# Attention and a max-out MoE layer in one kernel: batch 0 cut into two query parts, with MoE spans of 256 and 320 tokens

## The chip, the core and the metric

The kernel runs on one core of one Trainium2 chip. The metric is the device time of one execution in microseconds. Seven runs of the kernel before the change have a median of 294.08 us (293.69 to 296.04).

## What is computed

```python
def _attn_ref(q, k, v):                       # (8, 8, 576, 64) each: batch, head, sequence, dim
    scores = 1.0 / np.sqrt(D) * np.matmul(q, k.transpose(0, 1, 3, 2))
    mask = (pos[:, None] // 64) >= (pos[None, :] // 64)
    scores = np.where(mask, scores, -1000000000.0)
    attn = np.exp(scores - np.max(scores, axis=-1, keepdims=True))
    attn = attn / (np.sum(attn, axis=-1, keepdims=True) + 1e-09)
    return np.matmul(attn, v)

x = attn_out.transpose(0, 2, 1, 3).reshape(4608, 512)
g = np.maximum(x @ w1, x @ w2)                # w1, w2: (512, 1024)
out = g @ w_out                               # w_out: (1024, 512), out: (4608, 512)
```

The mask is causal by blocks of 64: a query sees all keys of its own block and of the blocks ahead of it. All inputs are float32; the kernel computes in bfloat16 with float32 accumulation.

## The kernel before

**Attention.** The heads of a batch are worked on two at a time: 4 pairs a batch, 32 pairs in all (`NPAIR`). Two pairs make a group g, and q and k of a group are loaded together (`load_qk`, L89, by SP), cast to bfloat16 (`cast`, L101), transposed on TensorE (`transposes`, L259) and copied out of PSUM into rings of four (`qT_r`, `kT_r`). For a pair, TensorE computes transposed scores (`scores`, L278: keys on partitions, queries in columns), 128 keys (a chunk, 5 in all) at a time and only for queries that can see them. ACT takes the exponential into `aT` (`exp`, L287). Where the first 64 queries of a chunk's columns must not see its last 64 keys, GpSimd writes zeros (`mask`, L292: 64 partitions, 2 x 64 elements; four a pair). `burst_a` (L295) and `burst_b` (L306) do the two halves of a pair; each uses two of the two buffers of the PSUM pool `ps_s`, so a score tile waits until ACT has read the one two before it. `CB` (L50) says where in `aT` a chunk begins.

`av` (L317) multiplies `aT` with V, which has a column of ones for the row sums, for some query tiles of 128 (tiles 0 and 1, or 2 to 4), and DVE divides by the sum (L339, L340). `x_out` (L345) transposes a group's result on TensorE, and DVE copies it into `xT` (L358, L359), the MoE's input with features on partitions. After a batch's second group `done_tokens` rises by 576.

**MoE.** Tokens are cut into 9 spans of 512. `h_unit(i, f)` (L159) computes 128 of the 1024 hidden features of span i: 4 matmuls with w1, a copy on DVE (L175), 4 with w2 and a maximum on DVE (L177). `y_unit` (L181) multiplies 128 tokens of the result g with w_out (8 matmuls), ACT copies it out (L192), and SP stores it. `y_last` does the last 128 tokens in halves. The PSUM pool `ps_m` has 4 buffers for everything but scores.

**Order.** The order on each engine is that in which the Python code issues (L70, `manual_schedule`); nothing is moved later. The MoE is a generator of single matmul steps (`moe`, L216). `fill(n)` (L245) takes up to n steps of it, but only those whose span lies within `done_tokens` (`needs`, `ready`). The main loop (L455) goes over pairs 4 to 31 and puts fills between the bursts; `fill_of` (L368) divides the steps that are ready, less 6, over the pairs until more come. AV of a pair follows two pairs later (`LAG`).

**The start** (L416 to L452). Batch 0 has no MoE beside it. Its four pairs run one after the other, with `warm_up` matmuls on zeros between (L251); then come AV of pairs 1 to 3, `x_out(0)` and `x_out(1)`. Only then is the first span ready. In the loop's first pass (s == HP) 6 steps, the transposes of group 2 and 6 more steps come first.

**Loads.** q and k of groups 0 to 2 are issued at once by SP (and ACT, for the first k). GpSimd issues what is cast on the way: five V chunks a batch (`load_v`, L107), w1 and w2 in quarters and a half (`load_w`, L118) and w_out (`load_wo`). q and k of later groups are gated: GpSimd first writes one column of the target (L94), and SP's load waits for that. So GpSimd's queue, which also holds masks and most casts (`pool_work`, L375), sets when they start.

Of the kernel before, what the change touches and what calls it, by code (L numbers as in the profile page):

```python
# [14 lines left out]
def kernel(  # L15
# [36 lines left out]
    APAD = 64  # L52
    NCH = 5

    SPAN = 512
    NSPAN = NTOK // SPAN

    wpool = ctx.enter_context(tc.tile_pool(name="wpool", bufs=1))
    ring = ctx.enter_context(tc.tile_pool(name="ring", bufs=1))
# [29 lines left out]
    def load_qk(g, queues, gated=False):  # L89
        b, u = divmod(g, GPB)  # L90
        for nm, src, queue in (("q", q, queues[0]), ("k", k, queues[1])):
            raws[nm, g] = t = raw.tile([P, 2, RPP * D], FP32, name=f"{nm}raw")
            if gated:
                nc.gpsimd.memset(t[:, 0, :1], 0.0)  # L94
            queue.dma_start(
                out=t[:],
                in_=src[b, 4 * u:4 * u + 4].rearrange(
                    "(s h) (p t) d -> (h p) s (t d)", h=2, t=RPP),
            )
# [15 lines left out]
    w2r = moe_w2.rearrange("(c p) f -> p c f", p=P)  # L115
    wor = moe_w_out.rearrange("(c p) f -> p c f", p=P)

    def load_w(f0, fw):  # L118
        for dst, src in ((w1_sb, w1r), (w2_sb, w2r)):
            nc.gpsimd.dma_start(out=dst[:, :, f0:f0 + fw], in_=src[:, :, f0:f0 + fw])  # L120

    def load_wo(c0, n):
        nc.gpsimd.dma_start(out=wo_sb[:, c0:c0 + n, :], in_=wor[:, c0:c0 + n, :])
# [8 lines left out]
    nc.vector.memset(zeros[:], 0.0)  # L132
    nc.scalar.activation(out=warm[:], in_=warm[:], func=AF.Exp)
    load_qk(1, (SP, SP))
    load_qk(2, (SP, SP))
    make_identity(nc, ident)
    for r in range(NV):
        nc.vector.memset(vv_r[r][:, :, :, D:D + 1], 1.0)
# [3 lines left out]
    for r in range(NA):  # L142
        nc.vector.memset(aT_r[r][BLK:, :, CB[4] + 512:], 0.0)
        nc.vector.memset(aT_r[r][:BLK, :, AW:], 0.0)
    cast("q", 0, ((dve, 0, 6), (pool, 6, RPP)))
    cast("k", 0, ((act, 0, 5), (dve, 5, RPP)))
    for c in range(3):
        load_v(0, c)
    cast("q", 1, ((pool, 0, RPP),))
    for c in range(3, NCH):  # L150
        load_v(0, c)
    load_w(0, 256)
    load_w(256, 256)


    done_tokens = [0]
# [1 line left out]

    def h_unit(i, f):  # L159
        if f == 0:  # L160
            g_tiles[i] = g_pool.tile([P, NFF, SPAN], BF16, name="g")
        g = g_tiles[i]
        t0 = i * SPAN
        ph = []
        for w_sb in (w1_sb, w2_sb):
            pt = ps_m.tile([P, SPAN], FP32, name="ps_h", tag="m")
            for c in range(NDM):
                nc.tensor.matmul(  # L168
                    pt[:], w_sb[:, c, f * P:(f + 1) * P], xT[:, c, t0:t0 + SPAN],
                    start=(c == 0), stop=(c == NDM - 1),  # L170
                )
                if c == NDM - 1:
                    if not ph:
                        h1 = h1_pool.tile([P, SPAN], BF16, name="h1")
                        nc.vector.tensor_copy(out=h1[:], in_=pt[:])  # L175
                    else:
                        nc.vector.tensor_max(g[:, f, :], h1[:], pt[:])  # L177
                    ph.append(pt)
                yield

    def y_unit(i, s):  # L181
        g = g_tiles[i]
        t0 = i * SPAN + s * P
        py = ps_m.tile([P, d_model], FP32, name="ps_y", tag="m")
        for f in range(NFF):
            nc.tensor.matmul(  # L186
                py[:], g[:, f, s * P:(s + 1) * P], wo_sb[:, f, :],
                start=(f == 0), stop=(f == NFF - 1),
            )
            if f == NFF - 1:  # L190
                y = y_pool.tile([P, d_model], FP32, name="y")
                nc.scalar.copy(out=y[:], in_=py[:])  # L192
                nc.sync.dma_start(out=out[t0:t0 + P, :], in_=y[:])
            yield

    def y_last(i, s):
        g = g_tiles[i]
        t0 = i * SPAN + s * P
        w = d_model // 2
        for h in range(2):  # L200
            py = ps_m.tile([P, w], FP32, name="ps_y", tag="m")
# [11 lines left out]
                            out=out[t0:t0 + P, h * w + m:h * w + m + w // 2], in_=y[:])  # L213
                yield

    def moe():  # L216
        ny = SPAN // P
        for i in range(NSPAN):
            need = (i + 1) * SPAN
            for f in range(NFF):  # L220
                yield from ((need, 0) for _ in h_unit(i, f))
                if i > 1 and f % 2 == 0:
                    yield from ((need, 0) for _ in y_unit(i - 1, f // 2))
            if i == 0:
                for s in range(ny):
                    yield from ((need, 0) for _ in y_unit(0, s))
        for s in range(ny - 1):
            yield from ((NTOK, 0) for _ in y_unit(NSPAN - 1, s))
        yield from ((NTOK, 0) for _ in y_last(NSPAN - 1, ny - 1))


    needs = []
    for i in range(NSPAN):
        needs += [(i + 1) * SPAN] * (2 * NDM * NFF + (SPAN // P * NFF if i != 1 else 0))
    needs += [NTOK] * ((SPAN // P + 1) * NFF)
    moe_steps = moe()
    at = [0]

    def ready():
        n = at[0]  # L240
        while n < len(needs) and needs[n] <= done_tokens[0]:
            n += 1
        return n - at[0]

    def fill(n):  # L245
        for _ in range(min(n, ready())):
            next(moe_steps)
            at[0] += 1


# [38 lines left out]
            out=aT_r[p % NA][:m, :, a0:a0 + w], in_=ps[:m, :, :w], func=AF.Exp, scale=scale,  # L289
        )  # L290

    def mask(p, a0):  # L292
        nc.gpsimd.memset(aT_r[p % NA][BLK:, :, a0:a0 + BLK], 0.0)  # L293

    def burst_a(p):  # L295
        u0 = ps_s.tile([P, 2, 512], FP32, name="ps_s", tag="s")
# [20 lines left out]
    def av(p, ts):  # L317
# [11 lines left out]
        for gi, t in enumerate(ts):  # L329
            for hh in range(2):  # L330
                for c in range(t + 1):
                    a0 = CB[c] + t * P
                    nc.tensor.matmul(  # L333
                        po[:, gi, hh, :], a[:, hh, a0:a0 + P], vv[:, c, h0 + 2 * hh, :],
                        start=(mm == 0), stop=(mm == n_mm - 1),
                    )
                    mm += 1
# [4 lines left out]
            rec[:, :n].to_broadcast([P, n, 2, D]),  # L342
        )

    def x_out(g):  # L345
        b, u = divmod(g, GPB)
        xp = xps.pop(g)
        pe = ps_m.tile([P, 2, NCH, BLK], BF16, name="ps_xe", tag="m")
        po = ps_m.tile([P, 2, NCH - 1, BLK], BF16, name="ps_xo", tag="m")
        for s in range(2):  # L350
            for t in range(NCH):
                src = xp[:, t, s].rearrange("p a d -> p (a d)")
                nc.tensor.transpose(pe[:, s, t, :], src[:BLK], ident[:BLK, :BLK])  # L353
                if t < NCH - 1:
                    nc.tensor.transpose(po[:, s, t, :], src[BLK:], ident[BLK:, BLK:])
        dst = xT[:, 2 * u:2 * u + 2, b * S:b * S + NCH * P].rearrange(
            "p s (t h w) -> p s t h w", h=2, w=BLK)
        nc.vector.tensor_copy(out=dst[:, :, :, 0], in_=pe[:])  # L358
        nc.vector.tensor_copy(out=dst[:, :, :NCH - 1, 1], in_=po[:])  # L359
        if u == GPB - 1:  # L360
            done_tokens[0] = (b + 1) * S

# [9 lines left out]

    def pool_work(s):  # L375
        g, i = divmod(s, 2)
        if s == 0:
            load_w(512, 512)
            load_qk(3, (SP, SP), gated=True)
        elif s == 1 or s == 2:  # L380
            pass
        elif s == 3:
            cast("q", 2, ((act, 0, RPP),))
            cast("k", 2, ((act, 0, RPP),))
            load_qk(4, (SP, SP), gated=True)
            for c in range(3):
                load_v(1, c)
            cast("q", 3, ((pool, 0, RPP),))
            cast("k", 3, ((pool, 0, RPP),))
            for c in range(3, NCH):  # L390
                load_v(1, c)
            load_wo(0, 4)
            load_wo(4, 4)
        elif s == 4:
            pass
        elif s == 5:
            load_qk(5, (SP, SP), gated=True)
# [24 lines left out]
    ck((0,))  # L422
    cq((1,))
    ck((1,))
    for s in range(HP):
        burst_a(s)
        if s == 0:
            cast("k", 1, ((dve, 0, RPP),))
            warm_up(4)
        elif s == 1:  # L430
            transposes("k", 1, (dve, dve))()
            warm_up(2)
        elif s == 2:
            av(0, [0, 1])
            warm_up(2)
        else:
            av(0, [2, 3, 4])
        burst_b(s)
        pool_work(s)
        if s == 0:  # L440
            transposes("q", 1, (dve, dve))()
            warm_up(2)
        elif s == 1:
            warm_up(4)
        elif s == 2:
            warm_up(3)
    for p in (1, 2, 3):
        av(p, [0, 1])
        av(p, [2, 3, 4])
        if p == 2:  # L450
            x_out(0)
    x_out(1)  # L452

    x_due = []
    for s in range(HP, NPAIR):  # L455
        g, i = divmod(s, 2)
        if x_due:
            x_out(x_due.pop())
        n = fill_of(s)
        if s == HP:  # L460
            fill(6)
            cq = transposes("q", 2, (dve, act))
            ck = transposes("k", 2, (dve, act))
            cq()
            ck()
            fill(6)
        burst_a(s)
        n_a = n // 2 if n > 12 else n * 2 // 5
        n_b = n // 6
# [5 lines left out]
        if s >= HP + LAG:  # L475
            p = s - LAG
            av(p, [0, 1])
            fill(n_b)
            av(p, [2, 3, 4])
            if p % 2:  # L480
                x_due.append(p // 2)
        else:
            fill(n_b)
        fill(n - n_a - n_b)
# [5 lines left out]
        av(p, [2, 3, 4])  # L490
        fill(11)
    x_out(NG - 1)
    fill(len(needs))

# [33 lines left out]
```

The softmax here doesn't subtract the row's maximum and nothing guards it: scores larger than these inputs give would overflow.

## Time and profile before

| | |
|---|---|
| median of 7 runs | 294.08 us |
| profiled execution | 294.02 us |
| its span | 292.2 us |
| TensorE clock granted | 1.0 of full speed |
| HBM read, written | 34.60 MB, 9.44 MB |
| L168 ps_h matmuls | 133.6 us busy, 379 ns each |
| L186 ps_y matmuls | 66.5 us busy |
| L288 exponentials | 99.1 us busy |
| L109 V loads issued by GpSimd | 33.7 us busy |

The span is the time from the first to the last instruction in one profiled execution; 1.8 us lie around it. Engines are named PE (TensorE matmul), PEld (its weight loads), DVE, ACT, POOL (GpSimd) and SP. Matmuls overlap, so the 379 ns of one is longer than the distance to the next. An arrow `<-` in square brackets names what ended an engine's idle time before an instruction. For a DMA, "to landing" is the time from its issue until its data is there.

### The profile page before, as it was taken

Reading aid. Unit: us, or ns where it says so; the run is one execution under the profiler, and the core shown is the slowest. Engines: PE = TensorE matmul, PEld = TensorE weight load, DVE = VectorE, ACT = ScalarE, POOL = GpSimd, SP = SyncE. Lnnn points to the kernel's source line nnn. Section 1 sums busy time; section 2 is a strip of 40 time slices with the busy share of each in tenths; the row PEclk is TensorE's granted clock in tenths of the full one; section 3 lists DMA queues with packets and bytes.
Section 4 is the critical chain, followed back from the end, with each engine's and each line's share of the span. In section 5 each row is a group of like instructions: output and inputs, shape, how many; then the busy total and the mean of one; then the engine's idle time right before and its main releaser. Section 6 shows DMA issues by size and latency. Waiting matters only on the chain.

```text
span 292.2 us, 7406 instructions
## 1 busy us (share of the span) xinstructions
PE 277.0 (95%) x3067; PEld 141.1 (48%) x3116; DVE 181.8 (62%) x363; ACT 140.2 (48%) x200; POOL 95.5 (33%) x236
## 2 busy tenths in 40 slices
PE   8787999999999999999999999999999999999995
PEld 3345445445554454544454455454545544444443
DVE  6717677547986676666565656666665766464530
ACT  3883687686655555554545555545555000101112
POOL 2956536625644443144324432443111000000000
PEclk9999999999999999999999999999999999999999
DMA  7999999968923792569556594465110111011104
GB/s 264 289 187 294 222 183 169 235 145 170 201 31 145 94 216 46 199 73 211 73 200 72 145 139 148 81 62 63 40 38 37 38 69 41 36 72 38 72 36 144
DMA packets 56081, 36.65 MB, mean 125 GB/s; under 512 B 38768, under 2 KB 43376, under 8 KB 56048
## 3 DMA queue, kind: packets, MB, share of 16 engines
q0 software_dynamic: 41728, 7.87, 34.1%
q1 hardware_dynamic: 13760, 27.60, 27.9%
q10 hardware_dynamic: 560, 0.72, 0.7%
q8 instruction: 24, 0.39, 0.5%
q14 instruction: 9, 0.07, 0.1%
HBM read 34.60 MB, written 9.44 MB: 151 GB/s over the span
## 4 chain that ended last, share of the span: by engine, by line
PE 90%; ACT 4%; DVE 3%; issue 2%; ACTq 0%
PE ps_h L168 42%; PE ps_y L186 20%; PE ps_o L333 11%; PE ps_s L282 8%; ACT aT L288 3%; PE ps_w L254 3%; PE ps_qT L265 2%; PE ps_kT L265 2%; PE ps_xe L353 2%; DVE xp L340 1%; PE ps_y L203 1%; DVE kT L272 1%; DVE xT L358 0%; DVE qT L272 0%; DVE rec L339 0%
## 5 line engine op out<-in xcount | busy, mean ns | idle before, releaser
L168 PE MATMUL ps_h<-xT,w_sb 128*128 128x512 bf16 x547 | 133.6, 379 | 3.5 <-issue 1.8
L288 ACT ACTIVATE aT<-ps_s 128x1024 bf16<-128x1024 f32 (+1 forms) x128 | 99.1, 832 | 53.5 <-PE ps_s L282 53.5
L168 PEld LDWEIGHTS <-w_sb 128*128 128x128 bf16 x576 | 51.8, 98 | 59.7 <-issue 6.1
L175 DVE CAST h<-ps_h 128x512 bf16<-128x512 f32 x72 | 49.7, 690 | 45.0 <-PE ps_h L168 44.1
L186 PE MATMUL ps_y<-wo_sb,g 128*128 128x512 bf16 x262 | 66.5, 379 | 1.0 <-issue 0.2
L293 POOL MEMSET aT<- 64x128 bf16 x128 | 23.5, 199 | 120.7 <-ACT aT L288 120.5
L192 ACT COPY y<-ps_y 128x512 f32<-128x512 f32 x35 | 20.5, 587 | 83.9 <-PE ps_y L186 56.8
L177 DVE TENSOR_TENSOR g<-h,ps_h 128x512 bf16<-128x512 bf16 x72 | 49.3, 684 | 10.2 <-PE ps_h L168 10.2
L333 PEld LDWEIGHTS <-aT 128*128 128x128 bf16 x960 | 33.6, 98 | 14.9 <-DVE xp L340 8.4
L333 PE MATMUL ps_o<-vv,aT 128*128 128x65 bf16 x960 | 39.7, 194 | 1.1 <-DVE xp L340 0.4
L186 PEld LDWEIGHTS <-g 128*128 128x128 bf16 x280 | 25.5, 98 | 27.9 <-issue 3.2
L282 PE MATMUL ps_s<-qT,kT 64*128 64x64 bf16 (+4 forms) x384 | 34.5, 275 | 3.3 <-ACT aT L288 3.2
L109 POOL DMA_DIRECT2D vv<-in_v_dram x40 | 33.7, 848 | 0.3 <-issue 0.3
L340 DVE TENSOR_TENSOR xp<-ps_o,rec 128x256 bf16<-128x256 f32 x64 | 31.4, 491 | 2.2
L282 PEld LDWEIGHTS <-kT 64*128 64x128 bf16 x384 | 16.5, 94 | 18.9 <-issue 13.2
L339 DVE RECIPROCAL rec<-ps_o 128x4 f32<-128x4 f32 x64 | 11.8, 184 | 18.9 <-PE ps_o L333 18.8
L105 POOL CAST qn<-qraw 128x1152 bf16<-128x1152 f32 (+1 forms) x15 | 17.1, 1137 | 4.6 <-DMA qraw<-in_q_dram 4.6
L272 DVE COPY qT<-ps_qT 128x576 bf16<-128x576 bf16 x17 | 12.8, 757 | 5.6 <-PE ps_qT L265 4.4
L105 POOL CAST kn<-kraw 128x1152 bf16<-128x1152 f32 x13 | 14.9, 1144 | 2.2 <-DMA kraw<-in_k_dram 1.4
L358 DVE COPY xT<-ps_xe 128x640 bf16<-128x640 bf16 x16 | 7.8, 490 | 12.5 <-PE ps_xe L353 12.1
L272 DVE COPY kT<-ps_kT 128x576 bf16<-128x576 bf16 x17 | 12.8, 756 | 4.3 <-PE ps_kT L265 3.3
L254 PE MATMUL ps_w<-zeros 128*128 128x512 bf16 x34 | 10.9, 451 | 1.8 <-DVE zeros L132 1.2
(39 smaller groups left out, 102.8 us busy)
## 6 DMA issues: line engine op xcount, KB each, us to landing
qraw<-in_q_dram SPq DMA_DIRECT2D x16, 576.0 KB, 4.4
out_dram<-y SPq DMA_DIRECT2D x35, 256.0 KB, 2.1
kraw<-in_k_dram SPq DMA_DIRECT2D x15, 576.0 KB, 6.1
vv<-in_v_dram POOLq DMA_DIRECT2D x32, 128.0 KB, 5.7
w_sb<-in_moe_w_dram POOLq DMA_DIRECT2D x4, 256.0 KB, 7.6
w_sb<-in_moe_w_dram POOLq DMA_DIRECT2D x2, 512.0 KB, 16.4
wo_sb<-in_moe_w_out_dram POOLq DMA_DIRECT2D x2, 512.0 KB, 12.2
kraw<-in_k_dram ACTq DMA_DIRECT2D x1, 576.0 KB, 5.6
```

Source lines behind the costliest of these rows:

```text
L105: copy(out=n[:, j0:j1], in_=t[:, j0:j1])
L109: nc.gpsimd.dma_start(out=vv_r[b % NV][:rows, c, :, :D], in_=v[b, :, c * P:c * P + rows, :].rearrange("h p d -> p h d"),)
L168: nc.tensor.matmul(pt[:], w_sb[:, c, f * P:(f + 1) * P], xT[:, c, t0:t0 + SPAN], start=(c == 0), stop=(c == NDM - 1),)
L175: nc.vector.tensor_copy(out=h1[:], in_=pt[:])
L177: nc.vector.tensor_max(g[:, f, :], h1[:], pt[:])
L186: nc.tensor.matmul(py[:], g[:, f, s * P:(s + 1) * P], wo_sb[:, f, :], start=(f == 0), stop=(f == NFF - 1),)
L272: copies[i](out=t[:, :S].rearrange("q (p j) -> q p j", j=RPP), in_=pts[i].rearrange("q j p -> q p j"),)
L282: nc.tensor.matmul(ps[:m, hh, col:col + w], kT[r, c * P:c * P + m], qT[r, q0:q0 + w], start=True, stop=True,)
L288: nc.scalar.activation(out=aT_r[p % NA][:m, :, a0:a0 + w], in_=ps[:m, :, :w], func=AF.Exp, scale=scale,)
L293: nc.gpsimd.memset(aT_r[p % NA][BLK:, :, a0:a0 + BLK], 0.0)
L333: nc.tensor.matmul(po[:, gi, hh, :], a[:, hh, a0:a0 + P], vv[:, c, h0 + 2 * hh, :], start=(mm == 0), stop=(mm == n_mm - 1),)
L340: nc.vector.tensor_mul(xp[:, ts[0]:ts[0] + n, :, p % 2], po[:, :, :, :D], rec[:, :n].to_broadcast([P, n, 2, D]),)
```

## The change

Batch 0's queries are cut at 256 (`QCUT`). For its four pairs the bursts are new: `burst_p` has queries 0 to 255 against chunks 0 and 1, `burst_q1` to `burst_q3` the other 320 queries. `aT` gets another layout for these pairs, which `a_col` gives to `av`. The start is written out as one list: all four pairs' first parts with `av` of tiles 0 and 1, `x_out` of tiles 0 and 1 for both groups, and then the second parts with `fill` between. The second-part AVs and `x_out` (tiles 2 to 4) follow, in part in the loop's passes for pairs 4 and 5.

The MoE spans become 256, 320, seven of 512, and 448 tokens. As 576 isn't a multiple of 128, g tiles are 64 wider, and GpSimd copies the last 64 tokens of a span into the next one's tile (`carry`). A step of a span that is narrower than 512 costs its share in `fill`.

Loads: k of group 2 is gated and issued after batch 0's V and w1, w2's second quarter; the first quarters of w1 and w2 stand between V chunks, with k of group 1 cast on GpSimd between them and q of group 1 on DVE (before: the other way round). Groups 2 and 3 are cast on GpSimd (group 2 before on ACT). The transposes of group 2 stand between the second-part bursts. Loads of groups 3 and 4, V of batch 1 and w_out are set into the new list. The masks of pairs 2 and 3's first parts are DVE's.

```diff
+    QCUT = 256
+    def a_col(p, c, t):
+        if p >= HP:
+            return CB[c] + t * P
+        late = t * P >= QCUT
+        return t * P + {
+            0: 384 - QCUT if late else 0, 1: 704 - QCUT if late else 256 - P,
+            2: 1024 - QCUT, 3: 1408 - 3 * P, 4: 1344 - 4 * P,
+        }[c]
...
-    NSPAN = NTOK // SPAN
+    spans = [(0, QCUT), (QCUT, S - QCUT)]
+    spans += [(t0, min(SPAN, NTOK - t0)) for t0 in range(S, NTOK, SPAN)]
+    NSPAN = len(spans)
+    carry = [t0 % P for t0, _ in spans]
+    tiles = [(carry[i] + w) // P for i, (_, w) in enumerate(spans)]
...
-    load_qk(2, (SP, SP))
+    load_qk(2, (SP, None))
...
-    cast("q", 0, ((dve, 0, 6), (pool, 6, RPP)))
+    cast("q", 0, ((dve, 0, 7), (pool, 7, RPP)))
     cast("k", 0, ((act, 0, 5), (dve, 5, RPP)))
-    for c in range(3):
+    for c in range(2):
         load_v(0, c)
-    cast("q", 1, ((pool, 0, RPP),))
-    for c in range(3, NCH):
-        load_v(0, c)
-    load_w(0, 256)
-    load_w(256, 256)
+    load_w(0, 256, (0,))
+    cast("k", 1, ((pool, 0, RPP),))
+    load_w(0, 256, (1,))
...
-            g_tiles[i] = g_pool.tile([P, NFF, SPAN], BF16, name="g")
+            g_tiles[i] = g_pool.tile([P, NFF, SPAN + BLK], BF16, name="g")
+            if carry[i]:
+                end = carry[i - 1] + spans[i - 1][1]
+                nc.gpsimd.tensor_copy(
+                    out=g_tiles[i][:, :, :carry[i]],
+                    in_=g_tiles[i - 1][:, :, end - carry[i]:end])
...
     def fill(n):
-        for _ in range(min(n, ready())):
-            next(moe_steps)
+        while n > 0 and at[0] < len(steps) and steps[at[0]][1] <= done_tokens[0]:
+            u, _, cost = steps[at[0]]
+            next(u)
+            n -= cost
             at[0] += 1
...
+    def burst_p(p):
+        burst(p, ((0, 0, QCUT), (1, P, QCUT - P)), 0)
+    def burst_q1(p):
+        burst(p, ((0, QCUT, 320), (1, QCUT, 192)), 384)
+    def burst_q2(p):
+        burst(p, ((1, 448, P), (2, QCUT, 320), (4, 512, BLK)), 896)
+    def burst_q3(p):
+        burst(p, ((3, 384, 192),), 1408)
+    def masks_p(p, eng=None):
+        for a in (0, 256):
+            mask(p, a, eng)
+    def masks_q(p, eng=None):
+        for a in (1024, 1408):
+            mask(p, a, eng)
...
-    for s in range(HP):
-        burst_a(s)
...
-    x_out(1)
+    cast("q", 1, ((dve, 0, RPP),))
+    burst_p(0)
+    masks_p(0)
+    burst_p(1)
+    warm_up(2)
+    masks_p(1)
+    for c in range(2, NCH):
+        load_v(0, c)
+    load_w(256, 256)
+    cq = transposes("q", 1, (dve, dve))
+    burst_q1(0)
+    ck = transposes("k", 1, (dve, dve))
+    for i in range(2):
+        cq((i,))
+        ck((i,))
+    load_qk(2, (None, SP), gated=True)
+    load_w(512, 512)
+    warm_up(3)
+    burst_p(2)
+    av(0, [0, 1])
+    burst_q3(0)
+    warm_up(2)
+    burst_p(3)
+    av(1, [0, 1])
+    masks_p(2, nc.vector)
+    masks_p(3, nc.vector)
+    burst_q2(0)
+    av(2, [0, 1])
+    warm_up(2)
+    burst_q1(1)
+    av(3, [0, 1])
+    x_out(0, 0, 2)
+    warm_up(2)
+    cast("q", 2, ((pool, 0, RPP),))
+    cast("k", 2, ((pool, 0, RPP),))
+    load_qk(3, (SP, SP), gated=True)
+    masks_q(0)
+    burst_q2(1)
+    x_out(1, 0, 2)
+    warm_up(2)
+    burst_q3(1)
+    masks_q(1)
+    for c in range(3):
+        load_v(1, c)
+    fill(2)
+    burst_q1(2)
+    transposes("q", 2, (dve, dve))()
+    fill(3)
+    burst_q2(2)
+    fill(3)
+    burst_q3(2)
+    masks_q(2)
+    for c in range(3, NCH):
+        load_v(1, c)
+    load_wo(0, 4)
+    av(0, [2, 3, 4])
+    fill(2)
+    burst_q1(3)
+    fill(3)
+    burst_q2(3)
+    transposes("k", 2, (dve, dve))()
+    fill(3)
+    burst_q3(3)
+    av(1, [2, 3, 4])
+    masks_q(3)
+    cast("q", 3, ((pool, 0, RPP),))
+    cast("k", 3, ((pool, 0, RPP),))
+    load_wo(4, 4)
+    load_qk(4, (SP, SP), gated=True)
+    fill(4)
 
-    x_due = []
+    x_due = [0]
     for s in range(HP, NPAIR):
...
-            x_out(x_due.pop())
+            x_out(x_due.pop(), QCUT // P if s < HP + 2 else 0)
         n = fill_of(s)
-        if s == HP:
-            fill(6)
-            cq = transposes("q", 2, (dve, act))
-            ck = transposes("k", 2, (dve, act))
-            cq()
-            ck()
-            fill(6)
         burst_a(s)
...
+        elif s == HP:
+            av(2, [2, 3, 4])
+            fill(n_b)
+            av(3, [2, 3, 4])
+            x_due.append(1)
```

## The prediction

> **What bounds the kernel now.** I read the page first, then the table of stretches, then the timeline of each engine between 6 and 50 us.
>
> ```profile
> PE 277.0 (95%) x3067; PEld 141.1 (48%) x3116; DVE 181.8 (62%) x363; ACT 140.2 (48%) x200; POOL 95.5 (33%) x236
> PEclk9999999999999999999999999999999999999999
> ```
>
> TensorE is the bound over the whole span, at full clock. From about 37 us it has no gaps to speak of, so a change of the start is worth only what it takes off TensorE's empty time there. The stretches (columns: length, then busy time and count for PE, PEld, DVE, ACT, POOL, then clock, DMA share, GB/s) show where that is:
>
> ```profile
> 6.80:12.00 5.20, 4.12 (x75) 2.09 (x75) 3.31 (x5) 4.21 (x7) 5.20 (x6) 1.00 1.19 364
> 12.00:18.00 6.00, 4.58 (x55) 2.24 (x55) 3.10 (x6) 5.11 (x9) 5.86 (x17) 1.00 2.21 153
> 18.00:24.00 6.00, 5.30 (x119) 4.02 (x118) 2.58 (x9) 5.66 (x9) 2.31 (x12) 1.00 1.30 247
> 24.00:32.00 8.00, 5.49 (x95) 3.18 (x96) 6.07 (x15) 1.83 (x3) 6.58 (x9) 1.00 1.13 294
> 32.00:40.00 8.00, 7.79 (x84) 3.65 (x86) 5.62 (x9) 6.21 (x8) 1.80 (x7) 1.00 2.04 171
> ```
>
> Until 24 us ACT's exponentials lead (5.11 of 6, 5.66 of 6 us) and part of TensorE's time is warm-up matmuls on zeros; from 24 to 32 us ACT is nearly idle and TensorE waits for DVE. The MoE begins only then. In the timeline (start, length, engine):
>
> ```profile
> 27.11 0.39 PE L168 MATMUL ps_h<-xT,w_sb 128*128 128x512 bf16 x1
> 28.09 1.02 PE L168 MATMUL ps_h<-xT,w_sb 128*128 128x512 bf16 x4 [0.59 <-DVE xT L359]
> 34.82 1.90 PE L168 MATMUL ps_h<-xT,w_sb 128*128 128x512 bf16 x8
> 36.65 0.61 PE L282 MATMUL ps_s<-qT,kT 64*128 64x512 bf16 x6
> ```
>
> The last line, scores of pair 5's first half, ends at 37.26. It is my checkpoint: the same program point exists after the change. Eight steps in 1.90 us give (1.90 - 0.38)/7 = 0.217 us a step; I call a step of 512 columns a unit. At the checkpoint before has done all of batch 0's attention and 6 + 6 + 15 = 27 units (ready 64 + 32 = 96, (96 - 6)/6 = 15 in pair 4).
>
> **What the Trainium skill says.** "TensorE: Matmul & The Clock Gate", table at its head: DVE, ACT and GpSimd take their queues strictly in order. The trace agrees: GpSimd's V loads at 29.6 stand behind a cast that waited 1.42 us for k. Same page, "Back-to-back issue gap": a warm matmul costs N/2.4 + 2.5 ns, so two of 256 columns cost what one of 512 does; the trace has 0.217 us for 512 and (1.91 - 0.27)/15 = 0.109 us for the 256 columns of L203. "DMA: Bandwidth & Descriptors", "Queues, rings and completion order": the DMA engines go round-robin between queues, a packet at a time. The trace agrees in part: at 21 to 32 us both kinds move together, but a load sent into running weight loads comes late:
>
> ```profile
> L95 SPq DMA_DIRECT2D qraw<-in_q_dram x1: 368/368/368, 17.4 to 17.4; - x1
> DMA to landing us min/median/max: 7.1/7.1/7.1
> 28.50 1.15 POOL L105 CAST kn<-kraw 128x1152 bf16<-128x1152 f32 x1 [1.42 <-DMA kraw<-in_k_dram]
> qraw<-in_q_dram SPq DMA_DIRECT2D x16, 576.0 KB, 4.4
> ```
>
> **The change, part by part.**
>
> *Arithmetic.* Scores stay 1600 columns a pair and head, AV the same matmuls. Exponentials of 768, 1024, 1024, 384 elements replace 1024, 1024, 1024, 128: with 1.02 us for 1024 and 0.26 for 128, 0.85 ns an element, that is 0.80 + 1.02 + 1.02 + 0.48 = 3.32 us against 3.33: nothing. MoE: 10 spans for 9; 64 more matmuls of the same total width, nothing by the 0.109 above. DVE gets 16 more evictions; at 256 columns I take 0.43 us (xp at 256 is 0.424; bounds 0.35, half of 0.69, and 0.69), two of them 0.86 beside 8 x 0.109 = 0.87 us of TensorE: hidden, just. At 0.69 DVE would add 0.5 us for each of span 0's 8 slices of d_ff, partly under attention. The eight carry copies on GpSimd (512 elements, estimate 0.5 us from 1.15 for 1152) stand ahead of masks that are wanted two pairs, over 10 us, later: nothing; without that cover 0.5 us each. Warm-ups 34 to 32, in idle time. The end, from the last scores to the last store, has the same units: nothing.
>
> *Early MoE.* Batch 0's first 256 tokens need only 0.80 + part of the other exponentials, so x_out of tiles 0 and 1 comes early. By hand: first scores as before at 8.8; pair 0 and 1 first parts to 10.75; q of group 1 cast on DVE (1.35 us, now ahead of its copies) to 10.15, transposed to 10.6; the four transposes' copies, 0.75 each, to 13.5; pairs 2 and 3's first parts to 14.9. Four masks of pairs 2 and 3 are DVE's now (0.11 each, as L144); they wait for that last exponential, with pair 2's reciprocal and product queued behind them, which need its AV anyway. AV and x_out(1) near 18.5, first MoE matmul near 19.3 (before 27.11). V is not late: its first chunk landed 13.3, when k of group 2 was still in the same stretch; with that load gone I take 12.8 for both chunks (14.3 at worst, 1.5 us that the later wait swallows). From 14.9 five exponentials (4 x 1.02 + 0.48 = 4.6 us) with a gap of 0.3 before each, as in before (1.5), reach 21.0; then a fill of 0.65 and a score tile, 0.3: TensorE would be at AV of pair 0's late tiles at 22.0, with 8 units done.
>
> *The new wait.* That AV needs the masks at columns 1024 and 1408, which now stand on GpSimd behind two casts of group 2, and k of group 2 is loaded only after a gate far down GpSimd's queue. Its queue, from rows of before: V 6.7 to 8.6 (two); w1 quarter 0.8, 9.4; cast k1 1.18 (k1 lands 9.25), 10.6; w2 quarter 0.8, 11.4; four masks 0.63, 12.0; V three 2.5, 14.5; two w loads 1.6, 16.1; gate 0.1; SP issues k2 at 16.3. Landing: between 4.4 us (median of all q loads) and 8.5 (a load behind another); 7.1 was q of group 3, sent into the same weight loads. I take 6.5: 22.8. Behind it in order: cast k 1.15, two gates 0.2, two masks 0.35: 24.5. So TensorE waits 24.5 - 22.0 = 2.5 us, and ACT too, since pair 3's scores are queued behind on TensorE. The second gate also moves q and k of group 3 from 17.4 to 24.0, V of batch 1 and wo behind that; q3 then lands near 30 and its cast ends near 31.4, just before its transposes at 31.9.
>
> *From 24.5 to the checkpoint.* TensorE's work: four late AVs 4 x 0.9 = 3.6; 13 units (2+3+3+4+1) 2.8; scores of pair 3's rest 0.95, pair 4 0.85, pair 5's first half 0.54; two transposes 0.75; two x_outs 0.6: 10.1 us. Waits on the path: AV of pair 1 for a PSUM buffer behind two k copies on DVE (2 x 0.75) 1.1; pair 4's second half for ACT to free score buffers 0.5 + 0.65, as pair 4 has only 1 unit to fill with (ready 12, (12 - 6)/6 = 1); x_out(1) for reciprocal and product, 0.6 of 0.85; 0.2 elsewhere: 3.1 us. Checkpoint at 24.5 + 13.2 = 37.7 with 21 units. Against before: 37.7 - 37.26 = 0.44 later, and 6 units x 0.217 = 1.3 us behind. Sum +1.7 us. After that both have work in every pair (84 units over 5 pairs, 16 a pair, 3.5 us + 3 of attention, above ACT's 3.3 + 0.6 + 0.6), so the loss stays.
>
> Against the profiled execution, 294.02 us (span 292.2 and 1.8 around it), 1.7 more is 295.7; the median of the runs is 294.08, 0.06 above: 295.8.
>
> **Rivals.**
> *k2 lands in time (faster).* Mechanism: the wait of AV pair 0 on its masks. For it: SP's queue is empty, the V chunks are small, and in the steady state such loads take 4.4 us: 20.7, masks at 22.4, wait 0.4, 2.1 us less. If also DVE's order costs nothing at AV pair 1 (1.1 us), the sum is 1.7 - 2.1 - 1.1 = -1.5: 292.6. It decides at a landing of about 20.8 together with that buffer; with the landing alone the time is 293.7, no change. Against: at 16.3 four w loads are queued, and q3 took 7.1 there.
> *Group 3 late as well.* q3 and k3 start 6.6 us later than before beside V and wo. If k2 takes 8.5 us (masks 2.0 later) or q3 lands 2 us late so that its transposes stall: 297.8. For: k3 took 10.6 us in before; against: w1 and w2 are through by about 26.
> *The start is hidden anyway.* TensorE only swaps warm-ups and waits for MoE steps and the thin pair 4 gives it all back: 294.1. It is the case between.
>
> **How the numbers follow.** Forecast 295.8, chance 0.45 (its own range 294.9 to 296.8). Faster rival 0.28; late group 3 0.12; no net change 0.15. Differences under 0.3% (0.9 us) are about what a measurement of this kernel can't tell from none. The forecast and group 3's case are slower, 0.57; the faster rival gives 0.27 to faster, its rest and the last case 0.16 to same. Range 292.6 to 297.9: low end from the faster rival, high end from the 8.5 us landing.
>
> **What would show it.** Right: first ps_h near 19 us; the AV of pair 0's late tiles idle for over 1.5 us until masks that follow the k cast; k2 landing at 22 to 23.5; pair 4 with gaps at its score tiles; pair 5's first scores near 37.7. Wrong: masks done before 22.4, or a checkpoint before 36, or a steady part from 80 to 240 us that changes its pace by more than 0.5 us, for which I see no cause.

## The result, and the profile after

After takes 297.17 us (median of 12 runs, 296.42 to 298.54) against 293.91 us of before beside it: ratio 1.0107, 95% interval 1.0091 to 1.0122. It is slower, as forecast, but by 3.26 us where I had 1.7. The profiled execution took 296.59 us with a span of 294.7, 2.5 more than the span of before, and that difference is what the readings below account for.

The page of after, its engine line and its clock line:

```profile
PE 278.9 (95%) x3147; PEld 146.8 (50%) x3192; DVE 186.1 (63%) x389; ACT 137.7 (47%) x196; POOL 101.3 (34%) x243
PEclk9997999999999999999999999999999999999999
```

The 7 in the fourth slice is new. The timeline of TensorE (start, length, line; in brackets the idle time ahead and what ended it):

```profile
18.47 0.61 PE L195 MATMUL ps_h<-xT,w_sb 128*128 128x256 bf16 x4
...
21.64 0.23 PE L401 MATMUL ps_o<-vv,aT 128*128 128x65 bf16 x2
25.00 0.84 PE L401 MATMUL ps_o<-vv,aT 128*128 128x65 bf16 x22 [3.12 <-POOL aT L333]
...
37.80 0.59 PE L322 MATMUL ps_s<-qT,kT 64*128 64x512 bf16 x5
```

The MoE begins 8.6 us earlier than before. At 21.64 TensorE reaches the AV of pair 0's late tiles, does two matmuls and stands for 3.12 us. GpSimd's timeline shows why:

```profile
23.46 1.15 POOL L127 CAST kn<-kraw 128x1152 bf16<-128x1152 f32 x1 [5.16 <-DMA kraw<-in_k_dram]
24.55 0.10 POOL L116 MEMSET qraw<- 128x1 f32 x1
24.74 0.62 POOL L333 MEMSET aT<- 64x128 bf16 x4
```

The masks are written from 24.74, behind a cast that waited 5.16 us for k of group 2. SP issued that load at 15.76; it took 7.5 us to land. The checkpoint, the end of pair 5's first scores, is 37.80 + 0.59 = 38.39, with 21 units done.

The table of stretches, in steps of 1 us, shows the 7 of the clock line from close by (the column ahead of the DMA share is the clock):

```profile
26.00:27.00 1.00, 1.00 (x9) 0.33 (x7) 0.96 (x3) 0.16 (x1) 1.00 (x2) 0.63 1.08 211
27.00:28.00 1.00, 1.00 (x6) 0.53 (x4) 0.20 (x1) 0.86 (x1) 1.00 (x3) 0.50 1.02 384
28.00:29.00 1.00, 1.00 (x25) 0.76 (x24) 0.23 (x1) 0.22 (x1) 1.00 (x3) 0.50 1.04 387
29.00:30.00 1.00, 1.00 (x14) 0.68 (x8) 0.75 (x2) 0.80 (x1) 1.00 (x3) 0.66 1.30 303
```

A little over a microsecond after the idle time, TensorE has half its clock: 0.74 + 1 + 1 + 0.68 = 3.42 us of it, so 1.7 us of its work is lost. The busy column reads 1.00 throughout; only the clock column betrays it. "TensorE: Matmul & The Clock Gate", "Part 1: The HAM clock gate", states a window of 3413 ns and a halved clock after at least one idle window. The length agrees; the trigger does not, since the idle time here, 3.12 us in all, is shorter than one window, and in the runs below shorter still.

The rest of the span, from the checkpoint on, in after and in before:

```profile
38.40:294.70 256.30, 248.63 (x2712) 129.72 (x2754) 161.17 (x318) 117.77 (x170) 77.33 (x192) 1.00 0.50 108
```

```profile
37.26:292.20 254.94, 246.73 (x2660) 125.26 (x2705) 158.83 (x305) 117.65 (x170) 72.52 (x184) 1.00 0.52 107
```

After needs 1.36 us more there and has 6 units more to do, 6 x 0.217 = 1.30. So the whole difference of 2.5 us is made in the first 38 us: a checkpoint 1.13 us later, 6 units fewer at it.

### The profile page after: what moved, and what is told of

Read it like the earlier page. It is cut to its first block, busy times and chain, and to the rows that moved or that the text cites. A ratio compares the mean times of both kernels' runs of the same rounds, so it can differ in the third digit from the quotient of the medians.

```text
span 294.7 us, 7615 instructions
## 1 busy us (share of the span) xinstructions
PE 278.9 (95%) x3147; PEld 146.8 (50%) x3192; DVE 186.1 (63%) x389; ACT 137.7 (47%) x196; POOL 101.3 (34%) x243
## 4 chain that ended last, share of the span: by engine, by line
PE 86%; DVE 6%; DMA 3%; issue 2%; ACT 1%; POOL 0%; DVEq 0%; POOLq 0%; ACTq 0%
PE ps_h L195 40%; PE ps_y L213 20%; PE ps_o L401 11%; PE ps_s L322 7%; DMA kraw<-in_k_dram 3%; PE ps_w L294 2%; PE ps_kT L305 2%; PE ps_qT L305 2%; DVE kT L312 2%; PE ps_xe L423 2%; DVE xp L408 1%; DVE qT L312 1%; ACT aT L328 1%; DVE g L204 1%; PE ps_y L230 1%
## 5 line engine op out<-in xcount | busy, mean ns | idle before, releaser
L195 PE MATMUL ps_h<-xT,w_sb 128*128 128x512 bf16 (+3 forms) x616 | 136.4, 359 | 2.6 <-issue 1.6
L328 ACT ACTIVATE aT<-ps_s 128x1024 bf16<-128x1024 f32 (+3 forms) x128 | 100.0, 832 | 65.8 <-PE ps_s L322 65.3
L195 PEld LDWEIGHTS <-w_sb 128*128 128x128 bf16 x640 | 58.1, 98 | 56.7 <-issue 6.4
L202 DVE CAST h<-ps_h 128x512 bf16<-128x512 f32 (+3 forms) x80 | 50.9, 636 | 44.3 <-PE ps_h L195 42.8
L204 DVE TENSOR_TENSOR g<-h,ps_h 128x512 bf16<-128x512 bf16 (+3 forms) x80 | 50.5, 631 | 9.7 <-PE ps_h L195 7.4
L322 PE MATMUL ps_s<-qT,kT 64*128 64x64 bf16 (+6 forms) x400 | 35.2, 274 | 1.2 <-ACT aT L328 1.0
L408 DVE TENSOR_TENSOR xp<-ps_o,rec 128x256 bf16<-128x256 f32 (+1 forms) x64 | 31.4, 491 | 2.2
L407 DVE RECIPROCAL rec<-ps_o 128x4 f32<-128x4 f32 (+1 forms) x64 | 11.8, 184 | 18.8 <-PE ps_o L401 18.8
L185 POOL COPY g<-g 128x512 bf16<-128x512 bf16 x8 | 4.9, 612 | 37.9 <-DVE g L204 37.8
L428 DVE COPY xT<-ps_xe 128x640 bf16<-128x640 bf16 (+2 forms) x18 | 8.1, 452 | 12.4 <-PE ps_xe L423 11.8
```

The costliest lines, as they stand in the source:

```text
L195: nc.tensor.matmul(pt[:, :w], w_sb[:, c, f * P:(f + 1) * P], xT[:, c, t0:t0 + w], start=(c == 0), stop=(c == NDM - 1),)
L202: nc.vector.tensor_copy(out=h1[:, :w], in_=pt[:, :w])
L204: nc.vector.tensor_max(g[:, f, m:m + w], h1[:, :w], pt[:, :w])
L322: nc.tensor.matmul(ps[:m, hh, col:col + w], kT[r, c * P:c * P + m], qT[r, q0:q0 + w], start=True, stop=True,)
L328: nc.scalar.activation(out=aT_r[p % NA][:m, :, a0:a0 + w], in_=ps[:m, :, :w], func=AF.Exp, scale=scale,)
L408: nc.vector.tensor_mul(xp[:, ts[0]:ts[0] + n, :, p % 2], po[:, :, :, :D], rec[:, :n].to_broadcast([P, n, 2, D]),)
```

## The experiments

My theory: the late masks make TensorE wait, the wait lowers the clock, and these two are the loss. The rival: the loads set the pace of the start, so that a wait taken away comes back at the next load. Before is 294.1 to 294.4 us in every set of these runs. e1 to e4, e6 and e7 have 4 or 5 runs each, the others 6 to 22. Checkpoints are ends of the same scores, and all variants of after have 21 units there.

**Moving the load of k.**

```
-    load_qk(2, (SP, None))
+    load_qk(2, (SP, SP))
...
-    load_qk(2, (None, SP), gated=True)
```

> The changed kernel with k of group 2 loaded at the start by SP, as before the change, and not behind GpSimd's gate. Theory A (the loss is the wait of AV of pair 0's late tiles on masks that stand behind the k cast, 3.1 us, and the lowered clock that follows it, about 1.7 us): the wait goes, the granted clock is 1.0 throughout, V comes 1.5 us later so AV of the first tiles starts about 1 us later, and the time is 293 to 294. Theory B (the thin pair 4 and the in-order start give back what is won; the wait only stands in for other idle time): 296 or more, with gaps elsewhere before pair 5. Theory C (narrow spans and carry copies cost): 296 to 297.

It took 295.76 us, ratio 1.0049 (1.0032 to 1.0066). The wait for masks is gone, and the first AVs of the kernel wait instead, for V:

```profile
13.38 0.25 PE L401 MATMUL ps_o<-vv,aT 128*128 128x65 bf16 x3 [0.89 <-DMA vv<-in_v_dram]
14.24 0.25 PE L401 MATMUL ps_o<-vv,aT 128*128 128x65 bf16 x3 [0.62 <-DMA vv<-in_v_dram]
```

The clock was 0.73 of full from 12 to 18 us and 0.70 from 18 to 24, and the first MoE matmul came at 22.39, not 18.47. So the gate does what it is for: k loaded at once costs V and the early start, yet less in sum than the gate costs. None of the three ranges holds 295.76: the wait went as theory A says, but the one for V and its half clock were not in it.

```
     load_w(0, 256, (1,))
+    load_qk(2, (None, SP), gated=True)
...
-    load_qk(3, (SP, SP), gated=True)
     masks_q(0)
...
     masks_q(1)
+    load_qk(3, (SP, SP), gated=True)
```

> The after kernel with k of group 2 gated straight behind w2's first quarter (issue near 11 in place of 15.8), so that it goes after the first V chunks and ahead of the later ones; q and k of group 3 gated behind the masks of pair 1 (near 21), and the casts of group 3 ahead of batch 1's V and w_out. My theory: k lands by 17, masks are written by 19.9, the late AV at 21.6 does not wait, the clock stays full, and the weights' second halves come in time since group 3 follows them: checkpoint near 35 with 21 units, 292.3 to 293.6, below the kernel before. Rival (loads are the limit: what is brought forward pushes something else back): a wait of 1 to 3 us appears at ps_h on w_sb, or at the AV on vv, and the time is 294.5 to 296.5.

The gate between the two places, issue at 11.0; group 3 is gated further back, and its casts stand ahead of batch 1's V and w_out (a line was added at the head, so line numbers are one higher there). 300.09 us, ratio 1.0194 (1.0174 to 1.0213). k was cast at 18.36 without a wait, but group 3's loads now ran beside the second halves of w1 and w2:

```profile
31.54 1.04 PE L196 MATMUL ps_h<-xT,w_sb 128*128 128x256 bf16 x4 [3.39 <-DMA w_sb<-in_moe_w_dram]
```

Half clock followed for 10.2 us. My expectation failed by 7 us, and the rival's held in kind, though its range too was low.

**Moving the cast behind the masks.**

```
     cast("q", 2, ((pool, 0, RPP),))
-    cast("k", 2, ((pool, 0, RPP),))
     load_qk(3, (SP, SP), gated=True)
...
     masks_q(1)
+    cast("k", 2, ((pool, 0, RPP),))
```

> The changed kernel with the one cast of k of group 2 put behind the second-part masks of pairs 0 and 1 on GpSimd; the load itself stays late. Theory A: AV of pair 0's late tiles no longer waits (3.1 us) and the clock stays at 1.0 (1.7 us), but the gates, V of batch 1 and the cast of q of group 3 stay where they are in time (cast q3 ends near 32.4), so that the transposes of group 3, which TensorE would reach near 28.5, wait 2 to 3 us: 294.5 to 295.5. If the lateness of k alone is what costs and not its place ahead of the masks, the transposes of k wait instead and the time stays at 296 to 297.

298.88 us, ratio 1.0155 (1.0129 to 1.0182). The late AV ran at 21.62 without a wait. But the gates of group 3 stood behind that cast as well and were now free at 18, and its 1.2 MB overtook the weights:

```profile
28.30 0.61 PE L195 MATMUL ps_h<-xT,w_sb 128*128 128x256 bf16 x4 [1.68 <-DMA w_sb<-in_moe_w_dram]
30.94 1.03 PE L195 MATMUL ps_h<-xT,w_sb 128*128 128x256 bf16 x4 [2.02 <-DMA w_sb<-in_moe_w_dram]
```

Here too 10.2 us of half clock followed. I had expected a wait at group 3's transposes; it came at the weights, since I had followed the cast and not the two DMAs behind it.

**The clock by itself.** Twelve matmuls on zeros ahead of the AV that waits; nothing else is touched.

```
+    warm_up(12)
     av(0, [2, 3, 4])
```

> The changed kernel with 12 matmuls on zeros ahead of AV of pair 0's late tiles: 2.6 us of TensorE work inside the 3.1 us wait, nothing else changed. If the lowered clock after the wait costs time (Theory A's second part): granted clock 1.0 between 25 and 30 us, 1.2 to 1.7 us less, 295.2 to 296.0, and the runs lie closer together. If the clock costs nothing on the path: 297 as in the changed kernel.

296.22 us, ratio 1.0056 (1.0036 to 1.0076); the profiled clock is 1.00 throughout 24 to 40 us, and what is left of the wait is 0.31:

```profile
24.89 0.84 PE L401 MATMUL ps_o<-vv,aT 128*128 128x65 bf16 x22 [0.31 <-POOL aT L333]
...
36.43 0.59 PE L322 MATMUL ps_s<-qT,kT 64*128 64x512 bf16 x5
```

Masks, loads and order are those of after: the AV goes on 0.11 us earlier, and the checkpoint, 37.02, is 1.37 earlier. So the drop from 1.0107, 0.5% or 1.5 us, is the clock: close to the 1.7 read off the stretches. Two of the five runs still have a clock of 0.992 and take 296.5; the other three, at 0.998 or more, take 295.25 to 296.22.

**The masks by themselves.** DVE writes the late masks of pairs 0 and 1; loads and casts stay.

```
-    masks_q(0)
+    masks_q(0, nc.vector)
...
-    masks_q(1)
...
+    masks_q(1, nc.vector)
     masks_q(2)
```

> The after kernel with only the four late masks of pairs 0 and 1 written by DVE in place of GpSimd, so that they no longer stand behind the cast of k of group 2; every load and cast keeps its place. My theory (the wait for these masks, and the half clock that follows it, are the loss): the 3.1 us idle time of the late AV at 21.6 goes, the clock stays at 1.00 from 25 to 31, but part of the gain is given back, since k of group 2 is cast only at 24.6 and q of group 3 only at 32.4 and TensorE now comes to their transposes early: 0.5 and some 2 us of waits there. 294.3 to 295.5. Rival (the loss is the late k itself, whoever writes the masks): TensorE only waits later, at the k transposes, as long as before: 296.4 to 297.4.

295.76 us, ratio 1.0044 (1.0023 to 1.0064). TensorE's timeline:

```profile
22.24 0.90 PE L401 MATMUL ps_o<-vv,aT 128*128 128x65 bf16 x24
...
28.82 0.61 PE L195 MATMUL ps_h<-xT,w_sb 128*128 128x256 bf16 x4 [1.09 <-DMA w_sb<-in_moe_w_dram]
...
31.94 0.66 PE L305 MATMUL ps_qT<-ident,qn 64*128 64x64 bf16 x18 [1.80 <-POOL qn L127]
```

The 3.12 us are gone, and 2.9 come back at two other places; the time lies between my range and the rival's. The clock column then reads 0.56, 0.50 five times, 0.53: 6.8 us of half clock from 31 on, two windows. The eight runs spread accordingly: 294.07 with a mean clock of 1.0, 296.39 to 296.54 with 0.987 or 0.988, four between (one of them 295.83 at 0.998, so the clock is not all of the spread). The one run at full clock is at the time of before.

> As the run before, and the two casts of group 3 on GpSimd moved ahead of the last V chunks of batch 1 and the first half of w_out. If the second wait is GpSimd's order, the q transposes of group 3 wait 1 to 1.5 us less: 293.3 to 294.6. If it is the landing of q of group 3 (issued at 24.7), they wait as long as in the run before, and the time is the same within 0.4 us.

e7 moves the casts of group 3 ahead of `load_v(1, 3)`, `load_v(1, 4)` and `load_wo(0, 4)`: 299.21 us, ratio 1.0158 (1.0137 to 1.0178). The q cast now waited for the landing (30.05), so landing, not order, was the limit there. The 3.4 us lost are another matter: the masks of pair 3 now stood behind the k cast of group 3 and the V loads after it.

```profile
31.25 0.44 PE L305 MATMUL ps_qT<-ident,qn 64*128 64x64 bf16 x18 [2.08 <-POOL qn L127]
...
36.00 1.39 PE L401 MATMUL ps_o<-vv,aT 128*128 128x65 bf16 x22 [3.17 <-POOL aT L333]
```

It is the mechanism of after once more, at another pair, by my own edit.

**Both causes together.** e5, with idle time filled: `warm_up(4)` ahead of `fill(4)` and `warm_up(8)` ahead of group 3's q transposes.

> As e5_masks_dve, with 4 warm-up matmuls ahead of the fill that waited for the weights and 8 ahead of the q transposes of group 3, so that the two idle times hold TensorE work that is worth nothing. If e5's spread (294.07 at clock 1.0, 296.5 at 0.988) is the clock that falls after idle TensorE: all runs at 0.998 or above, 294.0 to 294.6. If the clock falls for another reason: the same spread as e5, median 295.8 plus up to 0.5.

294.50 us (22 runs), ratio 1.0024 (1.0008 to 1.0039). Sixteen runs lie from 293.90 to 294.86 with clocks of 0.998 or more; four more reach 295.58 to 296.33 in that clock range, for which I have no reading, and two with 0.993 are above 297. So without the masks' wait and with the clock mostly held, 0.83 of the 1.07 points are gone: these two are most of the loss. The interval still excludes before. In the profiled run the checkpoint is 35.46, with the units counted 0.5 us ahead of before, although the two waits for loads are spent on zeros. What is lost comes behind it, most of it at the transposes of group 4's q:

```profile
43.06 0.44 PE L305 MATMUL ps_qT<-ident,qn 64*128 64x64 bf16 x18 [0.86 <-POOL qn L127]
```

**The spans alone.** Before, with only the new spans and carry copies.

> The kernel before with the MoE plan of the change alone: spans of 256, 320, seven of 512 and 448 tokens, wide g tiles and the carry copies on GpSimd; start, loads and batch 0's bursts as before. From the traces of both kernels after the checkpoint (256.3 against 254.9 us with 6 units of 0.217 more to do) the plan costs below 0.1 us: 293.9 to 294.3. Theory C (the plan costs): 295 to 297.

> The kernel before with only the MoE spans of 256 and 320 tokens and the carry copies, a second time on another chip. If its 1.2 us loss belongs to the spans: 295.2 to 295.9 and a ratio near 1.004 again, with the first q transposes late by 0.7. If it came from how the clock rose in those runs: 293.9 to 294.6, and a first transpose at the same time as in the kernel before.

295.53 us and, on another chip, 295.41: ratios 1.0043 (1.0028 to 1.0058) and 1.0036 (1.0023 to 1.0048). I had called this part free. In e4's profile the first transposes came 0.76 us late (7.55 for 6.79), in e8's only 0.16, with the same time, so that isn't it. This delay is the clock's: the record of full clock begins at 5.31 in before, 6.85 in e4 and 5.64 in e8, and the first ten warm-ups, which span 3.09 us in before, span 3.85 in e4 and 3.25 in e8. In e8:

```profile
34.34 0.61 PE L179 MATMUL ps_h<-xT,w_sb 128*128 128x256 bf16 x4 [0.22 <-DMA w_sb<-in_moe_w_dram]
...
37.57 0.61 PE L306 MATMUL ps_s<-qT,kT 64*128 64x512 bf16 x6
```

The checkpoint is 38.18 with 29 units: 0.92 later, of which 2 units are 0.43; the rest has the 0.16 and this 0.22 in it. Behind the checkpoint 0.6 us more are lost. The starts of the exponentials tell where: from pair 9 (57.87 in before, 60.67 in e8) to pair 31 (219.80 and 222.62) every pair comes 2.80 to 2.82 us later, with 8 units more done, which leaves the same 1.1 us all along. So the loss is made before 61 us, while the two narrow spans run, and the carry copies, the first of which starts at 68.9, have no part in it; which wait makes it I could not find. In after the stretch behind the checkpoint loses 0.06, so I do not add this cost to the loss of after; that it has no share in its first 38 us is not shown.

**Other work ahead of what is late.** e9 is e5 with TensorE's order changed: the late AV of pair 2 ahead of the fill that waited for weights, group 3's q transposes (first used by pair 6) behind the AV of pair 3, and the masks of pairs 2 and 3 on DVE.

```
     av(1, [2, 3, 4])
-    masks_q(3)
+    av(2, [2, 3, 4])
...
             fill(n_b)
             av(3, [2, 3, 4])
+            t_pair(s)()
```

> As e5_masks_dve (late masks of pairs 0 and 1 on DVE), and in addition the masks of pairs 2 and 3 on DVE, the late AV of pair 2 moved up ahead of the fill that waited 1.09 us for the weights' second half, and the q transposes of group 3 (which waited 1.80 us for the cast, and which pair 6 is the first to use) moved behind the late AV of pair 3. If the cause of the loss is that TensorE reaches work whose data are not there, while other work stands ready behind it: both waits are covered, the clock stays full, and 1.5 to 2.5 us come off the 294.1 that e5 took at full clock: 291.8 to 293.3, below the kernel before. If the loads as a whole set the pace (the rival): new waits of 1 to 2 us, 294.0 to 295.5.

296.49 us, ratio 1.0066 (1.0041 to 1.0090). The start did what I expected, the time did not: the checkpoint is 34.63, 2.63 ahead of before and 1.33 with the units counted. Then:

```profile
44.12 0.44 PE L305 MATMUL ps_qT<-ident,qn 64*128 64x64 bf16 x18 [2.75 <-POOL qn L127]
```

q of group 4 had been gated behind a cast that waited 2.24 us for the transposes that I had moved back. Half clock followed for 3.4 us (44 to 48). e11 takes `load_qk(4)` ahead of `cast("k", 3)`, e12 also moves pair 4's first scores and `x_out(0)` up, around the late AV of pair 2.

```
+    load_qk(4, (SP, SP), gated=True)
     cast("k", 3, ((pool, 0, RPP),))
```

> As e9_late_parts_up, with the gated load of q and k of group 4 moved on GpSimd's queue from behind the cast of k of group 3 and the second half of w_out to ahead of that cast (issue near 31 in place of 35). e9 had its start 1.3 us ahead of the kernel before (its checkpoint at 34.63 with 21 units), then lost 2.75 us to the transposes of q of group 4, whose load had been queued behind, and some 1.3 us to the half clock after it. If that is all: the wait goes, the clock stays full, 291.5 to 293.0. If loads as a whole are the limit there too: a wait of over 1 us shows at another load (k of group 3, V of batch 1 or w_out), 293.5 to 295.5.

293.82 us, ratio 0.9986 (0.9970 to 1.0002): not to be told from before, and by its number in the rival's range. The wait for group 4 is 0.17 in its profile, the clock 1.0, the span 291.2, 1.0 below before. Six of 14 runs have clocks of 0.993 or 0.994, at times (293.28 to 294.35) that overlap those of the others; one at 0.988 took 295.59.

```
     av(1, [2, 3, 4])
+    burst_a(HP)
     av(2, [2, 3, 4])
+    x_out(0, QCUT // P)
```

> As e11_group4_earlier, with the scores of pair 4's first half and x_out(0) moved up: the scores stand between the late AVs of pairs 1 and 2, so that ACT starts pair 4's exponentials near 27 in place of 29.7, and the fill of one unit's weights step stands where TensorE waited 0.98 us for a score buffer. If TensorE's last idle time of the start (1.5 us of waits for ACT in pair 4) is what is left to take and what still lowers the clock in half of e11's runs: 1 to 1.5 us less than e11's 293.8, 292.2 to 293.0, with most runs at 0.998 or above. If the clock falls whatever the order: 293.4 to 294.2.

293.06 us (22 runs), ratio 0.9960 (0.9946 to 0.9973): below both kernels, 19 of 22 runs at clocks of 0.998 or more. Its timeline:

```profile
32.81 0.59 PE L322 MATMUL ps_s<-qT,kT 64*128 64x512 bf16 x5
...
41.78 0.44 PE L305 MATMUL ps_qT<-ident,qn 64*128 64x64 bf16 x18 [1.64 <-POOL qn L127]
```

The checkpoint is 33.40, 3.86 ahead of before and 2.56 with the units counted; 1.64 goes back to q of group 4, which TensorE now reaches too early. That is the rival's share: as far as these runs go, the gain of the start is capped by the loads.

## Why the forecast was right in sign and short in size

- *TensorE bounds the steady part and only the start matters*: right. Behind the checkpoint after loses 0.06 us once the units are counted.
- *First MoE matmul near 19.3, late AV at 22.0*: 18.47 and 21.64. V's chunks came in time.
- *The new wait, 2.5 us*: right in mechanism, the masks behind the k cast of group 2, as written. The wait was 3.12: TensorE was there 0.36 earlier, and the masks let it go on at 25.00 for 24.5, since k was issued 0.5 earlier than my 16.3 but took 7.5 us for 6.5.
- *From 24.5 to the checkpoint 13.2 us*: 13.4 from 25.0, by errors that cancel. Half clock, 1.7 us, was not in the sum. TensorE's idle time was 1.9 us, 1.2 less than my 3.1: AV of pair 1 did not wait for a PSUM buffer (I had 1.1), while pair 4's score buffers (0.49 and 0.52 for 0.5 and 0.65) and `x_out(1)` (0.66 for 0.6) did as priced. The work without the half clock was 9.8 us for my 10.1. That the sum came out within 0.2 us is luck.
- *Checkpoint 37.7 with 21 units*: 38.39 with 21. The sum, +1.7, becomes +2.43: the later AV (25.0 for 24.5, 0.5) and the 0.2 above.
- *The step that failed* is the price of the wait: I took a wait of TensorE at its own length. It cost its length and then a window at half clock, 1.7 us. With that in it, and the other waits as I had them, the sum would be +3.4, too much for the profiled run (+2.5); so the forecast owes part of its nearness to a wait that never came. In 5 of 12 runs the mean clock is 0.987 or 0.988, which is two windows, in 7 it is 0.993 or 0.994, one; the first take 297.6 to 298.5, the others 296.4 to 297.2, their medians 1.4 apart. The profiled run is one of the latter, so the median is a further 0.58 above it.
- *The faster rival* (k in time): e1, e2 and e6 bring k or its masks in time and none is faster than before. The place of the wait was right, the assumption that nothing is late next was wrong.
- *Group 3 late as well*: hidden in after, since TensorE itself is late; with masks in time it is there, 1.80 us in e5. Its 297.8 is nearer to 297.17 than my 295.8, but not by its mechanism.
- *Spans and carry copies at nothing*: right for the copies, but before with the spans alone loses 1.1 us ahead of the first copy, about half of it to something I could not find.

## What to carry to other kernels

Price a wait of TensorE in a start with gaps at its length and, where some 1.6 us of idle time or more can fall within 3.4 us, at 1.4 to 1.7 us of half clock more (e11, where runs with one such piece were no slower, shows that it isn't always paid); ask what useful work could stand there, and only then what would shorten the wait. When loads set the pace, moving one load ahead moves another back (e1, e2 and e6 were all slower than before): instead let the engine that waits reach the late data later, with work that is ready put ahead. And before a mask or any small write is queued on an engine, look at what that engine's queue waits for ahead of it.

## What the runs showed of the hardware

- Half clock comes in pieces of one length: 3.42 us in after, 6.8 in e5, 3.4 in e9. In each of the 14 traces every change of the clock stands a whole number of 3.413 us behind the start of its first record at full clock (in after that starts at 5.79 and the drop is at 26.27, six lengths later), and this start itself lies anywhere from 4.51 to 7.22 us.
- Counted in these lengths, full clock was followed by half clock after each one in which TensorE's idle time came to 1.58 us (e1) or more, seven times in all, and after none with 1.55 us (e7) or less. Ends of matmuls are modelled in a profile, so the last digits are rough. In these runs it is thus not one wait's length that decides but the idle time that falls into one such length. In after the 3.12 us were cut into 0.98 and 2.15, and the drop came behind the second. In e5 1.09 and the first 0.97 of the 1.80 fell together, and half clock began within that wait. In e12 the 1.64 us were cut into 0.59 and 1.06, and the clock stayed. That the same kernel has one piece in some runs and two in others would follow from where the lengths begin relative to the waits; only one run of each has a trace, so this is not shown.
- A load of SP sent behind queued loads of GpSimd did not always share with them at once. In after, k was issued at 15.76, and by the packet records SP's queue moved nothing until 19.13; from 20 to 21 it moved 233 KB. In before, q of group 3, issued at 17.38, began at 21.03. Yet q of group 3 in after, issued at 24.68 with packets of weights still moving, began 1.08 us later. "DMA: Bandwidth & Descriptors", "Queues, rings and completion order", has the engines alternate between queues by packets; from 19 to 22 they did; for the 3 us ahead of that I have no explanation.
- `tensor_copy` on GpSimd of 128 x 512 bfloat16 took 0.61 us (I had estimated 0.5).
